# Which engine copies the first output bank out at the block boundaries of a Fourier layer fused with an ELU feed-forward

## The chip, the cores and the metric

The kernel runs on one core of a Trainium2 chip. The metric is device time in microseconds, the median of several executions. A core has TensorE (matrix products), VectorE, ScalarE and GpSimd (elementwise work), and SyncE, which here only issues DMAs. In the profile they are PE (with PEld for its weight loads), DVE, ACT, POOL and SP. [...]

## What is computed

A spectral layer on x (8 batches of 3008 tokens, 256 wide), followed by a feed-forward layer with an ELU (hidden width 2048):

```python
X = np.fft.rfft(x, axis=1)
Yr = Xr @ w_r - Xi @ w_i + b_r
Yi = Xr @ w_i + Xi @ w_r + b_i
Yr = np.sign(Yr) * np.maximum(np.abs(Yr) - 0.01, 0.0)   # Yi likewise
y = np.fft.irfft(Yr + 1j * Yi, n=3008, axis=1)

h = y @ w_in
g = np.where(h > 0.0, h, np.exp(np.minimum(h, 0.0)) - 1.0)
out = g @ w_out
```

## The kernel before

**Two streams of work in one loop.** The Fourier part of a batch is cut into some 38 "transform units": A and X (forward transform, the second after a trip through a scratch tensor in memory), M (the complex product and the soft threshold), B and Y (inverse transform, again with a scratch trip between them). The feed-forward layer of batch b is cut into 48 iterations: 6 blocks of 512 tokens (the last has 448) by 8 pairs of 128-wide slices of the hidden width. The main loop (line 826) runs over all 8 x 48 = 384 iterations, and each iteration of batch b also issues one transform unit of batch b+1 or b+2 as `plan` has laid it out. With r the iteration's number in its batch, an iteration without a unit is called `free` in the code; those are the last of each batch (r=41 among them) and nearly all of batch 7. The order of instructions on each engine is the order in which the code issues them; nothing reorders them later.

**One iteration i** issues, in this order:
1. its transform unit: matmuls into the PSUM tile `fps`, and a copy out of it, mostly by ScalarE (line 126). In an M unit, VectorE adds the bias (`yb`, line 196), and GpSimd does the soft threshold.
2. `front(i)`: four matmuls `hps` (line 688) into one of two PSUM tiles, the hidden activations of one pair for 512 tokens; then ScalarE computes the exponential into `Et` (line 701). Where the unit is an M unit (`on_act`), ScalarE does a Relu and an Exp instead (lines 698 and 699), which bound the exponential themselves.
3. `finish_elu()` for iteration i-1: one VectorE pass per pair gives `gT` from `hps` and `Et` (line 715, or 713 in the other form). It is the last reader of `hps`, so it frees that PSUM tile for `front(i+1)`, which is two iterations behind the one that it belongs to.
4. loads for later units (`f1`).
5. `elu(i)`: the minimum pass of VectorE over `Et` (line 726). There is none after Relu and Exp; in `free` iterations VectorE and GpSimd share it (line 724).
6. `back(i-2)`: eight matmuls (line 749) that add one pair's share of the output into two PSUM banks `ps_o`, the first four into the first bank, the other four into the second. When i-2 is the last pair of a block, `back` also copies both banks out into `osb` (line 763; line 767 for the short rows of the last block of a batch) and issues the output DMAs from SP (line 774).

**A block boundary** is thus an iteration i whose i-2 is the eighth pair of a block: r = 1, 9, 17, 25, 33 and 41, r=1 with the last block of the batch before. There are only two `ps_o` buffers, so the first matmuls of the next block, issued by `back(i-1)` one iteration later, must wait until the copies have emptied them. `osb` has two buffers as well; a copy into one waits until the output DMAs from two blocks earlier have read it.

At a boundary the units are, in batches 1 to 6: Y at r=1, X at r=9, M at r=17 and r=25, B at r=33. In batch 0 the list is one iteration later: X, B, Y, A at r = 9, 17, 25, 33. In batch 7 only r=1 has a unit.

Of the kernel before, what the change touches and what calls it, by code (L numbers as in the profile page):

```python
# [29 lines left out]
def kernel(  # L30
# [11 lines left out]
    nc = tc.nc  # L42
# [47 lines left out]
    NPAIR = NFT // 2  # L90
    NBLK = (S + TB - 1) // TB
    PER = NBLK * NPAIR
    LAG = 2
# [581 lines left out]
    def front(i, third, on_act):  # L675
        b, r = divmod(i, PER)
        blk, fp = divmod(r, NPAIR)
        bs = blk * TB
        nb = min(TB, S - bs)
        yT = yT_of[b]  # L680
        if third:
            hps = psF.tile([P, 2, TB], F32, name="hps", tag="fps")
        else:
            hps = psH.tile([P, 2, TB], F32, name="hps", tag="hps")
        for s in range(2):
            ft = 2 * fp + s
            for dt in range(2):
                nc.tensor.matmul(  # L688
                    hps[:, s, 0:nb], lhsT=w_in_s[:, dt, ft * P : ft * P + P],
                    rhs=yT[:, dt, bs : bs + nb], start=(dt == 0), stop=(dt == 1),  # L690
                )
        Et = late3.tile([P, 2, TB], F32, name="Et", tag="Et")
        E_ = Et[:, :, 0:nb]
        if i == n - 1:
            for s in range(2):
                nc.scalar.activation(E_[:, s], hps[:, s, 0:nb], AF.Exp)
        elif on_act:
            nc.scalar.activation(E_, hps[:, :, 0:nb], AF.Relu, scale=-1.0)  # L698
            nc.scalar.activation(E_, E_, AF.Exp, scale=-1.0)  # L699
        else:  # L700
            nc.scalar.activation(E_, hps[:, :, 0:nb], AF.Exp)  # L701
        return hps, Et, nb
# [3 lines left out]
    def finish_elu():  # L706
        for i, hps, Et, nb, whole in late_elu:
            E_, h_ = Et[:, :, 0:nb], hps[:, :, 0:nb]
            gT = late3.tile([P, 2, TB], F32R, name="gT", tag="gT")
            for s in range(2) if i == n - 1 else (slice(0, 2),):  # L710
                o, h, e = gT[:, s, 0:nb], h_[:, s], E_[:, s]
                if whole:
                    nc.vector.scalar_tensor_tensor(o, e, -1.0, h, ALU.add, ALU.max)  # L713
                else:
                    nc.vector.scalar_tensor_tensor(o, h, 0.0, e, ALU.max, ALU.add)  # L715
            g_of[i] = gT
        late_elu.clear()

    def elu(i, hps, Et, nb, on_pool, on_act):

        E_ = Et[:, :, 0:nb]
        if on_pool:
            for eng, s in ((nc.gpsimd, 1), (nc.vector, 0)):
                eng.tensor_scalar(E_[:, s], E_[:, s], 1.0, 0.0, ALU.min, ALU.max)  # L724
        elif not on_act:
            nc.vector.tensor_scalar(E_, E_, 1.0, -1.0, ALU.min, ALU.add)  # L726
        late_elu.append((i, hps, Et, nb, on_pool or on_act))

    def back(i):
        b, r = divmod(i, PER)  # L730
        blk, fp = divmod(r, NPAIR)
        bs = blk * TB
        nb = min(TB, S - bs)
        gT = g_of.pop(i)
        nsub = (nb + P - 1) // P
        if fp == 0:
            po_of[b, blk] = [
                psO.tile([P, 2, E], F32, name="ps_o", tag="outp") for _ in range((nsub + 1) // 2)
            ]
        po = po_of[b, blk]  # L740
        nq = (nsub + 1) // 2
        order = [(q, s) for q in range(nq) for s in range(2)]
        if i == n - 1:
            order = [(q, s) for s in range(2) for q in range(nq)]
        for q, s in order:
            ft = 2 * fp + s
            for i_ in range(2 * q, min(2 * q + 2, nsub)):
                t0, t1 = i_ * P, min(i_ * P + P, nb)
                nc.tensor.matmul(  # L749
                    po[q][0 : t1 - t0, i_ % 2, :], lhsT=gT[:, s, t0:t1],  # L750
                    rhs=w_out_r[:, ft, :], start=(ft == 0 and i_ % 2 == 0),
                    stop=(ft == NFT - 1), skip_group_check=True,
                )
        if fp < NPAIR - 1:
            return
        osb = late2.tile([P, 4, E], F32, name="osb", tag="osb")
        ov = out[b * S : b * S + S, :].rearrange("(r w j) e -> w r j e", w=4, j=8)
        last = i == n - 1
        for q in range(nq):
            k = min(2, nsub - 2 * q)  # L760
            copy = nc.vector.tensor_copy if last and q else nc.scalar.copy
            if nb >= (2 * q + k) * P:
                copy(osb[:, 2 * q : 2 * q + k, :], po[q][:, 0:k, :])  # L763
            else:
                for e in range(k):
                    rows = min(P, nb - (2 * q + e) * P)
                    copy(osb[0:rows, 2 * q + e, :], po[q][0:rows, e, :])
            for i_ in range(2 * q, 2 * q + k):
                t, end = bs + i_ * P, min(bs + i_ * P + P, bs + nb)
                while t < end:  # L770
                    w, r0 = t // WT, t % WT // 8
                    t1 = min(end, (w + 1) * WT)
                    p0, n8 = t - bs - i_ * P, (t1 - t) // 8
                    (nc.scalar if last and i_ % 2 == 0 else nc.sync).dma_start(
                        ov[w, r0 : r0 + n8], osb[p0 : p0 + 8 * n8, i_, :]
                    )
                    t = t1
        del po_of[b, blk]
# [4 lines left out]
    def plan(b):  # L783

        f0 = [[] for _ in range(PER)]
        f1 = [[] for _ in range(PER)]
        n1, n2 = b + 1, b + 2
        mid = [("X", u) for u in range(8)] + [
# [4 lines left out]
        ]  # L793
        if n1 < B:
            lead, seq = int(b == 0), [("y", u) for u in range(2, 6)] + mid
            seq.insert(20, ("y", 6))
            seq.insert(24, ("y", 7))
            xs = (3, 8, 13)
            yn = (45, 47)
        else:  # L800
            lead, seq = 0, [("y", u) for u in range(2, 8)]
        for t, u in enumerate(seq, lead):
            if u[0] == "y":
                f0[t].append(put("Y", b, u[1]))
            elif u[0] == "A":
                if n2 < B:
                    f0[t].append(put("A", n2, u[1]))
            else:
                f0[t].append(put(u[0], n1, *u[1:]))
            if u == ("A", 2):  # L810
                f1[t] += [(load_Bs, (n1, w)) for w in range(4)]
            if u == ("A", 5) and n2 < B:
                f1[t] += [(load_Z, (n2, s0, s1)) for s0, s1 in ((0, 8), (8, NS))]
        if b == 0:
            f1[xs[0]].append((lambda: gate(Z_of[1][:, 16, 0:1]), ()))
        if n2 < B:
            for ci in range(3):
                f1[xs[ci]].append((load_x, (n2, ci)))
        if n1 < B:
            for u in range(2):  # L820
                f0[yn[u]].append(put("Y", n1, u))
        return f0, f1
# [3 lines left out]
    for i in range(n + LAG):  # L826
        if i < n:
            r = i % PER
            if r == 0:
                f0, f1 = plan(i // PER)  # L830
                used = [bool(u0 or u1) for u0, u1 in zip(f0, f1)]
            free = not used[r]
            bare = bare + 1 if free else 0
            calm = free and (i >= n - 2 or (r + 2 < PER and not used[r + 1] and not used[r + 2]))
            for f, a in f0[r]:
                f(*a)
            on_act = any(f is unit_M for f, a in f0[r])
            h = front(i, calm and bare % 3 == 2, on_act)
        finish_elu()
        if i < n:  # L840
            for f, a in f1[r]:
                f(*a)
            elu(i, *h, free and i > 0, on_act)
        if i >= LAG:
            back(i - LAG)


# [28 lines left out]
```

## Time and profile before

| | |
|---|---|
| median of 3 executions | 930.38 us (930.08 to 931.6) |
| the profiled execution | 931.51 us |
| its span in the trace | 929.7 us |
| copies of line 763 on ScalarE | 88 of 128x512, 0.587 us on average |
| copies of line 767 on ScalarE, on VectorE | 14 on ScalarE, 2 on VectorE (last block) |
| granted TensorE clock | 0.998 |

The profile is a record of one execution. Its page gives the busy time of each engine and the costliest groups of instructions (line, engine, operation, output and inputs, count, then busy time and mean length in ns, then the idle time of the engine before them and what ended it). The list of waits names, for each engine and line, whose completion ended its idle time, in total, how often, and the longest. A timeline has the start in us from the beginning of the span, the length in us, the engine, the line, the operation, and in brackets the idle time of that engine in front of it with what ended it; neighbouring instructions of one kind are merged (x8), and their length is then from the first start to the last end. The ends of matmuls are modelled and they overlap, so that the distances between starts are the better measure on TensorE.

### The profile page before, as it was taken

The numbers are of one execution on the slowest core, as the hardware profiler recorded it, in microseconds if no ns is written. First come the engines' busy times: TensorE is split into PE (matmuls) and PEld (weight loads), VectorE is DVE, ScalarE is ACT, GpSimd is POOL, SyncE is SP. The second block draws the span as 40 slices with busy tenths as digits, with TensorE's granted clock in tenths as the row PEclk, the third lists the DMA queues.
The fourth block names the chain that finished last, engine by engine and source line by source line (L and its number), as shares of the span: only waits on it lengthen the run. The fifth ranks groups of instructions, "written<-read, shape, count | busy, mean of one in ns | idle before, by whom it ended". The sixth has DMA issues, their size and how long they took to land.

```text
span 929.7 us, 16768 instructions
## 1 busy us (share of the span) xinstructions
PE 909.2 (98%) x6583; PEld 644.4 (69%) x6583; DVE 734.5 (79%) x863; ACT 710.7 (76%) x818; POOL 267.9 (29%) x352
## 2 busy tenths in 40 slices
PE   8879999999999999999999999999999999999997
PEld 3447677776677666776677766777667766677775
DVE  7868778877788767886778877887778876888997
ACT  6657887787878788688787878778787878676654
POOL 6801441133310431205412153113331043321332
PEclk9999999999999999999999999999999999999999
DMA  8984216621383224722166021752138002421011
GB/s 264 353 254 136 91 47 187 196 69 46 95 223 111 69 65 126 224 84 86 51 181 202 24 91 46 222 161 68 47 94 224 22 24 63 116 51 43 23 46 43
DMA packets 90655, 106.21 MB, mean 114 GB/s; under 512 B 5264, under 2 KB 81296, under 8 KB 87216
## 3 DMA queue, kind: packets, MB, share of 16 engines
q1 hardware_dynamic: 84320, 77.61, 29.8%
q0 software_dynamic: 5968, 27.26, 8.9%
q8 instruction: 51, 0.84, 0.4%
q10 hardware_dynamic: 288, 0.26, 0.1%
q14 instruction: 28, 0.23, 0.1%
HBM read 55.31 MB, written 49.81 MB: 113 GB/s over the span
## 4 chain that ended last, share of the span: by engine, by line
PE 75%; DVE 14%; DMA 4%; ACT 4%; issue 1%; SPq 1%; DVEq 0%; POOL 0%; ACTq 0%; POOLq 0%
PE ps_o L749 30%; PE hps L688 29%; PE mps L189 8%; DVE gT L713 8%; DVE Et L724 3%; PE bps L238 2%; PE aps L143 2%; PE xps L174 2%; DMA Z<-DA 2%; DVE gT L715 1%; PE yps L276 1%; ACT Et L701 1%; DMA DA<-A 1%; DVE Et L726 1%; DMA xt<-in_x_dram 1%
## 5 line engine op out<-in xcount | busy, mean ns | idle before, releaser
L749 PE MATMUL ps_o<-w_out_r,gT 128*128 128x256 f32 (+1 forms) x3072 | 485.8, 301 | 0.8 <-DVE gT L713 0.5
L749 PEld LDWEIGHTS ps_o<-w_out_r,gT 128*128 128x128 f32 (+1 forms) x3072 | 406.4, 186 | 65.5 <-DVE gT L713 14.4
L688 PE MATMUL hps<-yT,w_in_s 128*128 128x512 bf16 (+1 forms) x1536 | 390.5, 376 | 5.4 <-DVE gT L715 2.7
L701 ACT ACTIVATE Et<-hps 128x1024 f32<-128x1024 f32 (+1 forms) x299 | 301.4, 1008 | 84.4 <-PE hps L688 80.4
L713 DVE SCALAR_TENSOR_TENSOR gT<-Et,hps 128x1024 fp32r<-128x1024 f32 (+2 forms) x187 | 219.9, 1176 | 62.9 <-ACT Et L699 41.6
L715 DVE SCALAR_TENSOR_TENSOR gT<-hps,Et 128x1024 fp32r<-128x1024 f32 (+1 forms) x198 | 240.1, 1213 | 17.6 <-DVE Et L726 0.9
L688 PEld LDWEIGHTS <-w_in_s 128*128 128x128 bf16 x1536 | 131.8, 98 | 141.0 <-issue 24.0
L726 DVE TENSOR_SCALAR Et<-Et 128x1024 f32<-128x1024 f32 (+1 forms) x198 | 136.0, 687 | 58.0 <-ACT Et L701 51.4
L204 POOL TENSOR_SCALAR clip<-yb 128x512 f32<-128x512 f32 x84 | 51.7, 615 | 335.1 <-DVE yb L196 234.5
L724 POOL TENSOR_SCALAR Et<-Et 128x512 f32<-128x512 f32 (+1 forms) x102 | 64.3, 630 | 271.1 <-ACT Et L701 269.9
L698 ACT ACTIVATE Et<-hps 128x1024 f32<-128x1024 f32 x84 | 86.4, 1029 | 70.0 <-PE hps L688 70.0
L205 POOL TENSOR_TENSOR Y<-yb,clip 128x512 bf16<-128x512 f32 x84 | 107.3, 1278 | 7.0
L196 DVE TENSOR_TENSOR yb<-mps,bias_bc 128x512 f32<-128x512 f32 x96 | 65.7, 687 | 39.3 <-PE mps L189 32.4
L699 ACT ACTIVATE Et<-Et 128x1024 f32<-128x1024 f32 x84 | 88.8, 1058 | 2.7
L126 ACT CAST yT<-yps 128x752 bf16<-128x752 f32 x63 | 49.7, 788 | 13.4 <-PE yps L276 13.4
L126 ACT CAST XT<-xps 128x768 bf16<-128x768 f32 x61 | 49.1, 807 | 13.7 <-PE xps L174 13.7
L189 PE MATMUL mps<-wcat_r,XT 128*128 128x512 bf16 x192 | 58.1, 384 | 0.6 <-ACT XT L126 0.6
L189 PE MATMUL mps<-wcat_s,XT 128*128 128x512 bf16 x192 | 57.1, 379 | 0.0
L126 ACT CAST A<-aps 128x1024 bf16<-128x1024 f32 x45 | 45.5, 1013 | 14.3 <-PE aps L143 11.9
L724 DVE TENSOR_SCALAR Et<-Et 128x512 f32<-128x512 f32 (+1 forms) x102 | 55.6, 545 | 0.4 <-ACT Et L701 0.2
L189 PEld LDWEIGHTS <-XT 128*128 128x128 bf16 x384 | 30.3, 98 | 29.5 <-ACT XT L126 0.9
L763 ACT COPY osb<-ps_o 128x512 f32<-128x512 f32 x88 | 47.2, 587 | 2.8 <-PE ps_o L749 2.8
(103 smaller groups left out, 398.5 us busy)
## 6 DMA issues: line engine op xcount, KB each, us to landing
xt<-in_x_dram POOLq DMA_DIRECT2D x21, 1024.0 KB, 5.2
out_dram<-osb SPq DMA_DIRECT2D x158, 128.0 KB
Bs<-DB SPq DMA_DIRECT2D x32, 384.0 KB
DA<-A SPq DMA_DIRECT2D x21, 512.0 KB
DB<-Bz SPq DMA_DIRECT2D x21, 512.0 KB
Z<-DA SPq DMA_DIRECT2D x7, 1152.0 KB
Z<-DA SPq DMA_DIRECT2D x11, 384.0 KB
xt<-in_x_dram POOLq DMA_DIRECT2D x6, 512.0 KB, 6.4
```

The source lines that it names most:

```text
L126: nc.scalar.copy(dst, src)
L189: nc.tensor.matmul(ps, lhsT=XT[:, dt, c, o : o + P], rhs=wm[:, dt, :], start=(m == 0 and dt == 0), stop=(m == 1 and dt == 1),)
L205: nc.gpsimd.tensor_tensor(Y_of[b, q][:, i, :], yb[:], clip[:], ALU.subtract)
L688: nc.tensor.matmul(hps[:, s, 0:nb], lhsT=w_in_s[:, dt, ft * P : ft * P + P], rhs=yT[:, dt, bs : bs + nb], start=(dt == 0), stop=(dt == 1),)
L698: nc.scalar.activation(E_, hps[:, :, 0:nb], AF.Relu, scale=-1.0)
L699: nc.scalar.activation(E_, E_, AF.Exp, scale=-1.0)
L701: nc.scalar.activation(E_, hps[:, :, 0:nb], AF.Exp)
L713: nc.vector.scalar_tensor_tensor(o, e, -1.0, h, ALU.add, ALU.max)
L715: nc.vector.scalar_tensor_tensor(o, h, 0.0, e, ALU.max, ALU.add)
L724: eng.tensor_scalar(E_[:, s], E_[:, s], 1.0, 0.0, ALU.min, ALU.max)
L726: nc.vector.tensor_scalar(E_, E_, 1.0, -1.0, ALU.min, ALU.add)
L749: nc.tensor.matmul(po[q][0 : t1 - t0, i_ % 2, :], lhsT=gT[:, s, t0:t1], rhs=w_out_r[:, ft, :], start=(ft == 0 and i_ % 2 == 0), stop=(ft = ...
```

## The change

At a boundary that is not `free`, and has a transform unit therefore, `back(i-2)` is issued before `elu(i)` and not after it, and its copy of the first bank goes to VectorE. The copies of the second bank stay on ScalarE. The boundaries of free iterations, and the first iterations, are as before.

```diff
-    def back(i):
+    def back(i, split):
...
-            copy = nc.vector.tensor_copy if last and q else nc.scalar.copy
+            copy = nc.vector.tensor_copy if (last and q) or (split and q == 0) else nc.scalar.copy
...
             for f, a in f1[r]:
                 f(*a)
+            split = not free and i > LAG and (i - LAG) % NPAIR == NPAIR - 1
+            if split:
+                back(i - LAG, True)
             elu(i, *h, free and i > 0, on_act)
-        if i >= LAG:
-            back(i - LAG)
+        else:
+            split = False
+        if i >= LAG and not split:
+            back(i - LAG, False)
```

By the instruction order of the two programs, the copies of 128x512 that move from ScalarE to VectorE are 35. On VectorE each stands directly behind the `gT` pass of iteration i-1, ahead of the minimum pass of i or, where there is none, ahead of the next `yb`. Of the instructions on TensorE, GpSimd and SP, the number and the order stay as they are.

## The prediction

> **What bounds the kernel now.** I read the page's busy times first, then the list of waits, then the timeline around the block boundaries.
>
> ```profile
> span 929.7 us, 16768 instructions
> ...
> PE 909.2 (98%) x6583; PEld 644.4 (69%) x6583; DVE 734.5 (79%) x863; ACT 710.7 (76%) x818; POOL 267.9 (29%) x352
> ...
> L763 ACT COPY osb<-ps_o 128x512 f32<-128x512 f32 x88 | 47.2, 587 | 2.8 <-PE ps_o L749 2.8
> ```
>
> TensorE sets the time. VectorE and ScalarE have some 20% free over the span, but an edit to either of them counts only where TensorE waits for it. So the question is which TensorE waits begin or end at the 35 boundaries where the new branch is taken.
>
> ```profile
> PEld ps_o L749 <- ACT osb L763: 7.7, 18, 0.5
> ...
> PE hps L688 <- DVE gT L715: 2.7, 10, 0.9
> ```
>
> These two rows of the list of waits matter (total, count, longest). In the first, the output matmuls of the next block wait until a copy has emptied the bank that they overwrite. In the second, the first matmuls of an iteration wait for the VectorE pass that frees their hidden bank. The first wait is what the change can remove; the second is what it can lengthen.
>
> The 35 boundaries are of three kinds. The branch is taken where the iteration's place r in its batch is 1, 9, 17, 25 or 33 (at 41 there is no transform unit), not in the last batch beyond r=1, and not at the very first r=1. That is 7 + 7 + 7 + 7 + 7. **Kind M:** r=17 and r=25 of batches 1 to 6, 12 boundaries, whose unit is an M; there ScalarE does Relu and Exp, and there is no minimum pass on VectorE. **Kind E (early):** all of r=1 and r=9, 14 boundaries with a Y or X unit. **The rest:** 9 boundaries. Below, i is the boundary iteration, which issues `back(i-2)` for the last pair of its block.
>
> **Kind M, where a wait goes away.** Timeline of one of them (columns: start, length, engine, line):
>
> ```profile
> 211.81 1.21 DVE L715 SCALAR_TENSOR_TENSOR gT<-hps,Et 128x1024 fp32r<-128x1024 f32 x1
> ...
> 213.34 1.03 PE L688 MATMUL hps<-yT,w_in_s 128*128 128x512 bf16 x4
> 213.61 0.69 DVE L196 TENSOR_TENSOR yb<-mps,bias_bc 128x512 f32<-128x512 f32 x1 [0.59 <-PE mps L189]
> 213.74 1.06 ACT L763 COPY osb<-ps_o 128x512 f32<-128x512 f32 x2
> 214.22 1.21 DVE L713 SCALAR_TENSOR_TENSOR gT<-Et,hps 128x1024 fp32r<-128x1024 f32 x1
> ...
> 214.36 1.02 PEld L749 LDWEIGHTS ps_o<-w_out_r,gT 128*128 128x128 f32 x8 [0.49 <-ACT osb L763]
> ...
> 216.06 0.55 PEld L688 LDWEIGHTS <-w_in_s 128*128 128x128 bf16 x4 [0.21 <-issue]
> ```
>
> ScalarE's two copies can only start at 213.74, behind Relu and Exp. The weight load of the next block starts at 214.36, some 0.04 us after the first copy ends (213.74 plus 0.59, the mean of L763). The second copy ends at 214.80, while the matmuls already run: the wait is for the first bank alone. What it costs TensorE is less than the 0.49 of the weight load, since matmuls are still running then. An iteration with the same kinds of work and no such wait gives the measure:
>
> ```profile
> 205.56 1.03 PE L688 MATMUL hps<-yT,w_in_s 128*128 128x512 bf16 x4
> ...
> 206.24 1.27 PE L749 MATMUL ps_o<-w_out_r,gT 128*128 128x256 f32 x8
> ...
> 207.98 0.55 PEld L688 LDWEIGHTS <-w_in_s 128*128 128x128 bf16 x4 [0.21 <-issue]
> ```
>
> From hidden matmuls to hidden matmuls it is 2.42 us there and 2.72 at the boundary: the wait costs 0.30.
>
> After the change the first bank's copy is on VectorE behind gT(i-1), which starts at 211.81. Passes of VectorE overlap by some 0.08 (213.61 + 0.69 is 214.30, and the next starts at 214.22), so a pass of 1.22 us is followed 1.14 after its start, and the copy starts at 212.95. Its price has no row of its own; the nearest are these, by line and form:
>
> ```profile
> L249 DVE CAST A<-bps 128x512 bf16<-128x512 f32 x1 | 0.7, 691 | 1.1 <-ACT A L248 1.1
> ...
> L767 DVE COPY osb<-ps_o 128x256 f32<-128x256 f32 x1 | 0.4, 424 | 0.8 <-PE ps_o L749 0.8
> ```
>
> L249 reads the same 128x512 of the same kind of bank and differs in its output type only; I take its 0.69. As a slot (start to the next start) that is 0.60 to 0.61, as 213.61 to 214.22 shows for the 0.69 us pass of L196. The bounds: from below 0.42, the copy of half the size, and from above 1.14, the slot of a pass over twice the columns.
>
> The copy then ends at 213.64, and the yb pass at 213.61 loses nothing (212.95 + 0.60 = 213.55). TensorE could start the output matmuls 0.68 after 213.34, as at 206.24: at 214.02, with the first bank already free. ScalarE's copy of the second bank ends at 213.74 + 0.59 = 214.33; the fifth of eight matmuls needs it at about 214.02 + 4 x 0.14 = 214.58 (0.14 being the pace of 8 matmuls in the 1.27 us row less one of about 0.3). So the wait goes and no other takes its place: 12 x 0.30 = 3.6 us gained.
>
> [...]
>
> **Kind E, where the copy stands in front of the minimum pass.** One r=1 boundary:
>
> ```profile
> 284.31 1.29 PE L749 MATMUL ps_o<-w_out_r,gT 128*128 128x256 f32 x8
> 284.40 1.23 DVE L715 SCALAR_TENSOR_TENSOR gT<-hps,Et 128x1024 fp32r<-128x1024 f32 x1
> ...
> 285.62 0.58 ACT L763 COPY osb<-ps_o 128x512 f32<-128x512 f32 x1
> ...
> 285.76 0.69 DVE L726 TENSOR_SCALAR Et<-Et 128x1024 f32<-128x1024 f32 x1
> 285.79 1.03 PE L688 MATMUL hps<-yT,w_in_s 128*128 128x512 bf16 x4
> 286.09 0.64 ACT L767 COPY osb<-ps_o 128x256 f32<-128x256 f32 x2
> ...
> 286.56 1.22 DVE L715 SCALAR_TENSOR_TENSOR gT<-hps,Et 128x1024 fp32r<-128x1024 f32 x1
> 286.62 0.80 ACT L126 CAST yT<-yps 128x752 bf16<-128x752 f32 x1
> 287.29 1.04 ACT L701 ACTIVATE Et<-hps 128x1024 f32<-128x1024 f32 x1
> ...
> 287.59 0.51 PE L276 MATMUL yps<-M,Bs 96*128 96x94 bf16 x8
> ...
> 287.93 1.03 PE L688 MATMUL hps<-yT,w_in_s 128*128 128x512 bf16 x4
> ...
> 288.36 0.69 DVE L726 TENSOR_SCALAR Et<-Et 128x1024 f32<-128x1024 f32 x1 [0.58 <-ACT Et L701]
> ...
> 289.00 1.03 ACT L701 ACTIVATE Et<-hps 128x1024 f32<-128x1024 f32 x1
> 289.16 1.23 DVE L715 SCALAR_TENSOR_TENSOR gT<-hps,Et 128x1024 fp32r<-128x1024 f32 x1
> 289.75 0.52 PE L174 MATMUL xps<-M,Z 96*128 96x96 bf16 x8
> ...
> 290.30 0.68 DVE L726 TENSOR_SCALAR Et<-Et 128x1024 f32<-128x1024 f32 x1
> 290.44 1.02 PE L688 MATMUL hps<-yT,w_in_s 128*128 128x512 bf16 x4 [0.18 <-DVE gT L715]
> ```
>
> The bank is complete in time: four of the eight matmuls at 284.31 are done before 285.0, while VectorE is in gT(i-1). The copy starts at 284.40 + 1.14 = 285.54 (289.16 to 290.30 is this 1.14), the minimum pass at 286.14 instead of 285.76, and everything behind it on VectorE, first gT(i), is 0.38 later: gT(i) ends at 288.16 instead of 287.78. It frees the bank for the hidden matmuls two iterations on, which start at 287.93, only 0.15 behind it; a pass that is waited for is followed 0.05 after its end (289.16 + 1.23 to 290.44). So these matmuls start at 288.21: 0.28 lost. r=9 has the same gap:
>
> ```profile
> 193.49 1.22 DVE L715 SCALAR_TENSOR_TENSOR gT<-hps,Et 128x1024 fp32r<-128x1024 f32 x1
> ...
> 194.86 1.03 PE L688 MATMUL hps<-yT,w_in_s 128*128 128x512 bf16 x4
> ```
>
> 14 x 0.28 = 3.9 us lost.
>
> Against this stands what leaves ScalarE. Today its two copies push the yT cast to 286.62 and Exp(i+1) to 287.29, the minimum pass behind it waits 0.58, and gT(i+1) ends so late that the hidden matmuls at 290.44 stall. They come 0.69 after the transform unit at 289.75, against 0.34 without a stall (287.59 to 287.93): 0.35 lost. With one copy fewer (its slot is 286.09 - 285.62 = 0.47) Exp(i+1) could start at 286.82, and not before 286.86, 1.07 after its matmuls (287.93 to 289.00). It ends at 287.90; VectorE is free at 286.94 + 1.14 = 288.08, so gT(i+1) starts 0.80 later, at 288.88, and ends at 290.11, ahead of the 290.38 at which TensorE, itself 0.28 late, wants the bank (290.44 - 0.34 + 0.28). This stall is gone. It follows all seven r=1 boundaries and the r=9 of batch 0 (8 of the 10 in the second row of the waits); after the other r=9 an M unit covers it. 8 x 0.34 = 2.7 us gained.
>
> **What costs nothing.** At r=33 VectorE idles before the minimum pass:
>
> ```profile
> 253.51 0.69 DVE L726 TENSOR_SCALAR Et<-Et 128x1024 f32<-128x1024 f32 x1 [0.42 <-ACT Et L701]
> ...
> 255.98 1.04 PE L688 MATMUL hps<-yT,w_in_s 128*128 128x512 bf16 x4
> ```
>
> Of the 0.60 slot some 0.5 falls into that idle time and the 0.08 of overlap, and gT(i), ending at 255.53 (253.51 + 0.80 + 1.22), has 0.45 before it is missed. Without this cover each would lose like kind E, 9 x 0.28 = 2.5. The wait in front of the copy gets longer, since it must also know that the old output DMAs of its buffer have landed; ScalarE's copy carries the same conditions today and started at 285.62 without idling. Extra conditions show up as short instructions of VectorE's queue:
>
> ```profile
> L767 DVEq EVENT_SEMAPHORE  x4: 49/50/50, 923.1 to 923.3; - x4
> ```
>
> ```profile
> 922.98 1.15 DVE L713 SCALAR_TENSOR_TENSOR gT<-Et,hps 128x448 fp32r<-128x448 f32 x2
> ```
>
> They ran beside the passes in front of them, so I take nothing for them; exposed, three of them would add 0.15 at each E boundary, 2.1 us. TensorE's, GpSimd's and SP's orders do not change: scratch writes, loads and output DMAs follow each other as now, and no copy ends more than a few hundredths later than today (at the r=1 boundary 285.54 + 0.69 = 286.23 against 285.62 + 0.58 = 286.20), so no output DMA is held up.
>
> **The sum.** 3.9 - 3.6 - 2.7 = -2.4 us. It is made against the profiled execution, whose span of 929.7 us lies in an execution of 931.51, 1.1 above the median of 930.38; on the median it gives 928.0.
>
> **The rivals.**
> First, **the copy fits** at kind E, because Exp(i) ends later than VectorE's free time suggests or the copy's slot is near the lower bound of 0.42, with 0.20 of delay and 0.10 lost. Then 1.4 - 3.6 - 2.7 = -4.9: 925.5; with no loss at all -6.3: 924.1. Against it: VectorE goes from gT(i-1) to the minimum pass with 0.22 to spare at most.
> [...]
> Third, **the wait at kind M stays**, because the first output matmul waits for both banks and the second still comes from ScalarE at 214.33. Then only kind E counts: 3.9 - 2.7 = +1.2, 931.6, no change. Against it: matmuls began at 214.36 with the second copy still running.
> Fourth, kind E loses and **the stall at 290.44 stays**, because the delay on VectorE passes on to gT(i+1): 3.9 - 3.6 = +0.3, 930.7.
>
> **How the numbers follow.** The forecast 0.48, the copy fits 0.17, slower 0.15, the wait at M stays 0.08, the stall stays 0.12. About 0.2%, 1.9 us, is what a measurement can tell from no change: faster ends at 928.5. The forecast's own spread, by a slot 0.05 shorter to 0.10 longer, is -3.1 to -1.0: two thirds of it is faster, 0.33, and with the copy that fits 0.50. The rest of the forecast, the stall and the wait at M give 0.34 for no change; slower takes 0.16. The range goes from the copy that fits, 925.0, to just above the third rival, 932.0; it leaves out most of the slower case and the largest gain.
>
> **What would show it.** Right: L763 splits into some 53 copies on ScalarE and 35 on VectorE of about 0.69 us; the wait of ps_o L749 for L763 falls from 18 to 6, those of the last batch; TensorE waits for gT L715 about 14 times instead of 8, one iteration earlier (near 288.2 instead of 290.4); minimum passes at r=1 and r=9 start 0.38 later behind gT(i-1). Wrong: a copy on VectorE far from 0.69, idle VectorE in front of it, or hidden matmuls at r=3 and r=11 that do not wait.

## The result, and the profile after

The changed kernel takes 926.49 us (926.0 to 927.33, 5 runs) against 930.66 for the kernel before (930.08 to 931.97, 5 runs): a ratio of 0.9953, with a 95% interval of 0.9940 to 0.9967. That is 4.2 us faster, inside the predicted range and in the predicted direction, where -2.4 us had been forecast. The profiled execution of the changed kernel took 927.22 us, with a span 4.3 us shorter than before. Its page begins:

```profile
span 925.4 us, 16719 instructions
...
PE 898.0 (97%) x6477; PEld 643.8 (70%) x6583; DVE 754.0 (81%) x898; ACT 697.3 (75%) x783; POOL 268.3 (29%) x352
```

VectorE has 35 instructions more and ScalarE 35 fewer. (PE has 6477 records against 6583 weight loads: 106 matmul records are missing.) The view of line 763 in the changed kernel (least, median and greatest length in ns, first and last start):

```profile
L763 ACT COPY osb<-ps_o x53: 566/585/607, 81.6 to 920.5; 128x512 f32<-128x512 f32 x53
L763 DVE COPY osb<-ps_o x35: 680/681/683, 81.5 to 831.9; 128x512 f32<-128x512 f32 x35
```

The copy's price was taken from a related pass as 0.69 us; it is 0.681 on VectorE, against 0.585 for the copies that stay on ScalarE. The two rows of the list of waits that the prediction started from are now:

```profile
PEld ps_o L749 <- ACT osb L763: 1.7, 5, 0.4
...
PE hps L688 <- DVE gT L715: 1.4, 2, 0.9
```

The waits for the bank went from 18 to 5, all of them at boundaries of free iterations, which the change does not touch. The waits for gT fell from 10 to 2.

**An M boundary after the change** (timeline):

```profile
212.71 0.68 DVE L763 COPY osb<-ps_o 128x512 f32<-128x512 f32 x1
...
213.11 1.03 PE L688 MATMUL hps<-yT,w_in_s 128*128 128x512 bf16 x4
213.38 0.69 DVE L196 TENSOR_TENSOR yb<-mps,bias_bc 128x512 f32<-128x512 f32 x1
...
213.51 0.57 ACT L763 COPY osb<-ps_o 128x512 f32<-128x512 f32 x1
213.76 1.10 PEld L749 LDWEIGHTS ps_o<-w_out_r,gT 128*128 128x128 f32 x8
...
215.53 0.55 PEld L688 LDWEIGHTS <-w_in_s 128*128 128x128 bf16 x4 [0.21 <-issue]
```

VectorE's copy ends at 213.39, before the weight load of the next block at 213.76, which has no wait in brackets any more. From the hidden matmuls to the weight load of the next ones it is 2.42 us instead of 2.72.

**An r=1 boundary after the change** (timeline, VectorE and TensorE with ScalarE's copy and Exp):

```profile
283.35 1.23 DVE L715 SCALAR_TENSOR_TENSOR gT<-hps,Et 128x1024 fp32r<-128x1024 f32 x1
...
284.50 0.68 DVE L763 COPY osb<-ps_o 128x512 f32<-128x512 f32 x1
284.60 0.63 ACT L767 COPY osb<-ps_o 128x256 f32<-128x256 f32 x2
...
284.74 1.03 PE L688 MATMUL hps<-yT,w_in_s 128*128 128x512 bf16 x4
285.09 0.68 DVE L726 TENSOR_SCALAR Et<-Et 128x1024 f32<-128x1024 f32 x1
...
285.81 1.23 DVE L715 SCALAR_TENSOR_TENSOR gT<-hps,Et 128x1024 fp32r<-128x1024 f32 x1
285.81 1.03 ACT L701 ACTIVATE Et<-hps 128x1024 f32<-128x1024 f32 x1
...
286.56 0.51 PE L276 MATMUL yps<-M,Bs 96*128 96x94 bf16 x8
...
287.09 1.02 PE L688 MATMUL hps<-yT,w_in_s 128*128 128x512 bf16 x3
...
288.89 0.52 PE L174 MATMUL xps<-M,Z 96*128 96x96 bf16 x8
...
289.24 1.03 PE L688 MATMUL hps<-yT,w_in_s 128*128 128x512 bf16 x4
```

Copy and minimum pass start 1.15 and 1.74 after the start of gT(i-1) at 283.35, as worked out (1.14, and 1.14 + 0.60). gT(i) ends at 287.04, and the hidden matmuls start 0.05 later, at 287.09, which is 0.53 after their transform unit instead of 0.34: they waited. The list of waits doesn't show it, because the modelled end of the unit's matmuls (286.56 + 0.51 = 287.07) covers the gap. From 284.74 to 287.09 it is 2.35 us, before 2.14 (285.79 to 287.93): 0.21 lost. From there to the next hidden matmuls, the stall of the kernel before is gone: 2.15 us (287.09 to 289.24) against 2.51 (287.93 to 290.44), 0.36 gained. All seven r=1 boundaries show this pair, 0.19 to 0.20 lost and 0.33 to 0.37 gained.

### The profile page after: what moved, and what is told of

Read it like the earlier page. It is cut to its first block, busy times and chain, and to the rows that moved or that the text cites. A ratio compares the mean times of both kernels' runs of the same rounds, so it can differ in the third digit from the quotient of the medians.

```text
span 925.4 us, 16719 instructions
## 1 busy us (share of the span) xinstructions
PE 898.0 (97%) x6477; PEld 643.8 (70%) x6583; DVE 754.0 (81%) x898; ACT 697.3 (75%) x783; POOL 268.3 (29%) x352
## 4 chain that ended last, share of the span: by engine, by line
PE 72%; DVE 16%; ACT 3%; issue 3%; DMA 3%; POOL 1%; SPq 0%; DVEq 0%; ACTq 0%; POOLq 0%
PE ps_o L749 29%; PE hps L688 28%; PE mps L189 8%; DVE gT L713 7%; DVE Et L724 3%; PE bps L238 2%; DVE gT L715 2%; ACT Et L701 2%; PE yps L276 2%; PE aps L143 2%; DVE Et L726 2%; PE xps L174 1%; DMA Z<-DA 1%; DMA DA<-A 1%; DMA xt<-in_x_dram 1%
## 5 line engine op out<-in xcount | busy, mean ns | idle before, releaser
L688 PE MATMUL hps<-yT,w_in_s 128*128 128x512 bf16 (+1 forms) x1463 | 383.5, 375 | 8.6 <-DVE gT L715 1.4
L715 DVE SCALAR_TENSOR_TENSOR gT<-hps,Et 128x1024 fp32r<-128x1024 f32 (+1 forms) x198 | 240.3, 1214 | 15.5
L189 PE MATMUL mps<-wcat_s,XT 128*128 128x512 bf16 x183 | 55.2, 379 | 1.1
L189 PE MATMUL mps<-wcat_r,XT 128*128 128x512 bf16 x171 | 53.5, 385 | 0.7 <-ACT XT L126 0.6
L251 ACT CAST Bz<-bps 128x1024 bf16<-128x1024 f32 x46 | 45.9, 999 | 3.2 <-PE bps L238 3.2
```

Source lines behind the costliest of these rows:

```text
L189: nc.tensor.matmul(ps, lhsT=XT[:, dt, c, o : o + P], rhs=wm[:, dt, :], start=(m == 0 and dt == 0), stop=(m == 1 and dt == 1),)
L688: nc.tensor.matmul(hps[:, s, 0:nb], lhsT=w_in_s[:, dt, ft * P : ft * P + P], rhs=yT[:, dt, bs : bs + nb], start=(dt == 0), stop=(dt == 1),)
```

## The experiments

Two theories were put against each other first. P is the prediction's: TensorE gains where it waited for the first bank, and loses or gains by small amounts where the copy stands ahead of the minimum pass. R: what counts is ScalarE's relief, an equal share for each copy that leaves it. All ratios are to the kernel before, with a 95% interval. The diffs are against the changed kernel.

**e1, the M boundaries alone.**

```diff
             split = not free and i > LAG and (i - LAG) % NPAIR == NPAIR - 1
+            split = split and on_act
```

> VectorE copies the first bank at the 12 boundaries with an M unit alone; the other 23 are as before. Theory P (the prediction's): each of the 12 gives back the 0.30 us for which TensorE waited on the bank, -3.6 us, about 927.1, and the wait of ps_o L749 for L763 falls from 18 to about 6. Theory R (the gain is ScalarE's relief, an equal share of the 4.2 us for each of the 35 copies moved): 12 x 0.12 = -1.4 us, about 929.2.

Measured: 927.39 us, ratio 0.9965 (0.9951 to 0.9978). The row of the list of waits falls as with the whole change:

```profile
PEld ps_o L749 <- ACT osb L763: 1.5, 5, 0.4
```

Twelve moved copies bring 3.3 us of the 4.2. P holds; R's 1.4 is far off.

**e2, the boundaries r=1 and r=9 alone.**

```diff
             split = not free and i > LAG and (i - LAG) % NPAIR == NPAIR - 1
+            split = split and r in (1, 9)
```

> The new order and VectorE's copy at r=1 and r=9 alone. Theory P: eight boundaries lose 0.2 us and give back the 0.35 us stall three iterations on, six lose 0.2 us and give nothing back: 8 x -0.15 + 6 x 0.22 = +0.1 us, no change, about 930.8; the 12 waits for L763 at M boundaries stay. Theory R: 14 x 0.12 = -1.7 us, about 929.0.

Measured: 930.43 us, ratio 0.9995 (0.9987 to 1.0004): fourteen moved copies bring nothing. List of waits:

```profile
PEld ps_o L749 <- ACT osb L763: 7.6, 17, 0.5
...
PE hps L688 <- DVE gT L715: 1.2, 2, 0.9
```

The 12 waits for the bank at M boundaries are all among the 17, and the eight stalls on gT are gone all the same; what they gave back was lost at the boundary. Loss and gain cancel, as P has it.

**e3, the change without r=9 of batches 1 to 6,** the boundaries that lose and give nothing back.

```diff
             split = not free and i > LAG and (i - LAG) % NPAIR == NPAIR - 1
+            split = split and not (r == 9 and i > PER)
```

> The change without the six r=9 boundaries of batches 1 to 6. Theory P: they are where it loses, 6 x 0.22 us; without them -4.2 - 1.3 = -5.5 us, about 925.2, some 1.3 us better than the change. Theory R: six copies fewer, -4.2 + 0.7 = -3.5 us, about 927.2.

Measured: 926.03 us, ratio 0.9947 (0.9934 to 0.9959). The direction is P's, but the times differ too little from the change's for the intervals to tell them apart. In the traces the loss is plain. The changed kernel at r=9:

```profile
192.27 1.03 PE L688 MATMUL hps<-yT,w_in_s 128*128 128x512 bf16 x4
...
194.63 1.02 PE L688 MATMUL hps<-yT,w_in_s 128*128 128x512 bf16 x4
```

and the kernel before, whose second row (194.86) the prediction shows:

```profile
192.72 1.03 PE L688 MATMUL hps<-yT,w_in_s 128*128 128x512 bf16 x4
```

It is 2.36 us against 2.14: 0.22 lost. In e3, where the copy is back on ScalarE, it is 2.15:

```profile
191.14 1.03 PE L688 MATMUL hps<-yT,w_in_s 128*128 128x512 bf16 x4
...
193.29 1.03 PE L688 MATMUL hps<-yT,w_in_s 128*128 128x512 bf16 x4
```

The same 0.22 us is saved in each of batches 1 to 6.

**e4, the other bank.** VectorE copies the second bank and ScalarE the first.

```diff
-            copy = nc.vector.tensor_copy if (last and q) or (split and q == 0) else nc.scalar.copy
+            copy = nc.vector.tensor_copy if (last and q) or (split and q == 1) else nc.scalar.copy
```

> Same order, but VectorE copies the second bank (or its short rows) and ScalarE the first. Theory P: at the M boundaries ScalarE's copy of the first bank still begins behind Relu and Exp, so the 12 waits of ps_o L749 for L763 stay with 0.49 us each, and only what happens at the other boundaries is left: -0.5 us, about 930.1. Theory R: the same number of copies leaves ScalarE, -4.2 us, about 926.5, as with the change.

Measured: 929.2 us, ratio 0.9981 (0.9972 to 0.9989), between the two. But P's reason failed: the 12 waits did not stay. Timeline of an M boundary of e4:

```profile
213.08 0.68 DVE L763 COPY osb<-ps_o 128x512 f32<-128x512 f32 x1
...
213.89 0.57 ACT L763 COPY osb<-ps_o 128x512 f32<-128x512 f32 x1
214.13 1.10 PEld L749 LDWEIGHTS ps_o<-w_out_r,gT 128*128 128x128 f32 x8
```

ScalarE's copy runs to 214.46, and the next block begins at 214.13 without a wait. The built program says why: at M boundaries its first output matmul waits for VectorE, the fifth for ScalarE.

```
L749 Matmult ps_o_2642<-w_out_r_65,gT_2605 128x256 [waits DVE_49]
L749 Matmult ps_o_2643<-w_out_r_65,gT_2605 128x256 [waits Activation_49]
```

The pool gave the next block the bank that VectorE had copied as its first. Which bank is "first" is thus not fixed by the kernel's code, but by the pool when the program is built. What e4 lost against the change was at r=1 and r=9: 0.37 and 0.30 us from start to start, where the change loses 0.20 and 0.22. Two things may make the difference, which no run tried apart: the second bank is complete later (at the r=1 boundary shown above, the eighth output matmul ends at 284.56, the fourth at 284.09), and at r=1 its short rows are two copies (of 128x256 and 64x256, 0.38 us each by the median on ScalarE in the kernel before). In e5 the pool can't choose.

**e5, e4 with fixed banks.**

```diff
-        tc.tile_pool(name="psO", bufs=2, space=bass.MemoryType.PSUM, reuse_waits="tile")
+        tc.tile_pool(name="psO", bufs=1, space=bass.MemoryType.PSUM, reuse_waits="tile")
...
-                psO.tile([P, 2, E], F32, name="ps_o", tag="outp") for _ in range((nsub + 1) // 2)
+                psO.tile([P, 2, E], F32, name="ps_o", tag=f"outp{q}") for q in range((nsub + 1) // 2)
```

> As e4 (VectorE copies the second bank, ScalarE the first), but each of the two banks has a pool of its own with one buffer, so that the first bank of the next block is always the one that ScalarE copied. Theory P with a pool that hands out whichever bank is released first: in e4 the next block at an M boundary began in VectorE's bank, so the wait was gone there too; with fixed banks it comes back, 12 x 0.30 = +3.6 us over e4's 929.2, about 932.8, and the waits of ps_o L749 for L763 are 17 or 18 again. Theory R (ScalarE's relief is what counts): as e4, about 929.2.

Measured: 932.14 us, ratio 1.0014 (1.0005 to 1.0023), 2.9 us above e4 and slower than the kernel before. The list of waits and the M boundary of e5:

```profile
PEld ps_o L749 <- ACT osb L763: 7.5, 17, 0.5
```

```profile
213.63 0.57 ACT L763 COPY osb<-ps_o 128x512 f32<-128x512 f32 x1
214.25 1.00 PEld L749 LDWEIGHTS ps_o<-w_out_r,gT 128*128 128x128 f32 x8 [0.49 <-ACT osb L763]
```

The wait is back with its old 0.49 us, and the time with it. From start to start, e5 is slower than e4 by 0.27 to 0.28 us at each of the 12 M boundaries, and after the first iterations nowhere else by as much as 0.1, so the fixed banks cost nothing of their own. As many copies leave ScalarE as in the change, so R is out: what counts is that the bank in which the next block begins is emptied early.

**e6, the same copies behind the minimum pass.**

```diff
-            if split:
-                back(i - LAG, True)
             elu(i, *h, free and i > 0, on_act)
+            if split:
+                back(i - LAG, True)
```

> VectorE copies the first bank at the same 35 boundaries, but behind its minimum pass. Theory P: nothing changes at the M boundaries (-3.6 us). Where there is a minimum pass the copy starts 0.60 behind it, some 286.36 in the r=1 boundary of the trace before, ends at 287.04, and the next block's matmuls, due at 286.47, wait 0.6 for the bank; less the 0.35 stall that goes at eight boundaries, it is 8 x 0.25 + 6 x 0.6 + 9 x 0.45 = +9.7 us, together +6 us, about 936.7. Rival: only the time that the copy takes on VectorE counts, not its place: within 0.5 us of the change, 926.5.

Measured: 928.6 us, ratio 0.9983 (0.9974 to 0.9992). Neither: 2 us worse than the change, and 8 better than worked out. Timeline at r=1:

```profile
284.01 0.69 DVE L726 TENSOR_SCALAR Et<-Et 128x1024 f32<-128x1024 f32 x1
...
284.62 0.68 DVE L763 COPY osb<-ps_o 128x512 f32<-128x512 f32 x1
284.69 1.19 PEld L749 LDWEIGHTS ps_o<-w_out_r,gT 128*128 128x128 f32 x8
```

The copy has hardly begun, and the next block starts without a wait. The pool again: in the built program of e6 the next block begins in ScalarE's bank at all 23 boundaries that have a minimum pass, and in VectorE's at the 12 others. (In the changed kernel it is VectorE's at all 35.)

**e9, e6 with fixed banks** (the pool as in e5).

> As e6 (VectorE's copy behind its minimum pass), with a pool of one buffer for each of the two banks, so that the next block must begin in the bank that VectorE copies. If e6 lost little only because the pool gave the next block ScalarE's bank first, the wait that was worked out for e6 comes now: some 0.3 us more than in e6 at 14 boundaries and 0.4 at nine, +8 us over e6's 928.6, about 936.6, and about 23 waits of ps_o L749 for VectorE's L763. Rival (the place of the copy doesn't matter): as e6, 928.6.

Measured: 934.93 us, ratio 1.0041 (1.0027 to 1.0055), 6.3 us above e6. List of waits, then r=1, both of e9:

```profile
PEld ps_o L749 <- DVE osb L763: 17.1, 23, 1.1
```

```profile
286.70 0.68 DVE L763 COPY osb<-ps_o 128x512 f32<-128x512 f32 x1
...
287.44 0.99 PEld L749 LDWEIGHTS ps_o<-w_out_r,gT 128*128 128x128 f32 x8 [0.78 <-DVE osb L763]
```

The 23 waits are the 14 + 9 that were counted; 8 us over e6 had been expected. So the place ahead of the minimum pass does matter, as long as the next block begins in VectorE's bank; and e6 lost little because the pool moved it.

**e7, less VectorE time behind the copy:** at r=1 and r=9 GpSimd takes half of the minimum pass.

```diff
-            elu(i, *h, free and i > 0, on_act)
+            elu(i, *h, (free and i > 0) or (split and r in (1, 9)), on_act)
```

> The change, and at r=1 and r=9 GpSimd takes half of the minimum pass (line 724), as in free iterations. Theory P: the loss there is the 0.2 us by which gT(i) ends late; VectorE's half is some 0.2 us shorter than the whole pass, and GpSimd's half (0.63 us from the end of Exp) is done by then, so gT(i) starts about 0.2 earlier: 14 x -0.2 = -2.8 us against the change, about 923.7. Rival: GpSimd's half ends later than VectorE's whole pass did, and nothing or a little is lost, 926.5 to 928.

Measured: 925.49 us, ratio 0.9948 (0.9935 to 0.9960): by the medians 1.0 us below the change, by the intervals not apart from it. Timeline at r=1:

```profile
283.22 0.61 POOL L724 TENSOR_SCALAR Et<-Et 128x512 f32<-128x512 f32 x1 [5.70 <-ACT Et L701]
283.55 0.56 DVE L724 TENSOR_SCALAR Et<-Et 128x512 f32<-128x512 f32 x1
...
284.21 1.22 DVE L713 SCALAR_TENSOR_TENSOR gT<-Et,hps 128x1024 fp32r<-128x1024 f32 x1
```

Half the columns took VectorE 0.56 us here. Without GpSimd beside it such a pass took 0.42 in batch 7 of e8:

```profile
852.09 0.42 DVE L724 TENSOR_SCALAR Et<-Et 128x512 f32<-128x512 f32 x1
```

The 0.2 expected had taken GpSimd's half to be done when VectorE's begins. It was not: it ran to 283.83, and VectorE's half, begun at 283.55, ended 0.28 after that. Of the 0.12 that is saved (0.56 against 0.68), half is lost again in front of gT(i), which in the built program waits for GpSimd and VectorE now, with a queue instruction of 21 ns for the second wait. The view of line 713 between 283 and 286 us:

```profile
L713 DVEq EVENT_SEMAPHORE  x1: 21/21/21, 284.1 to 284.1; - x1
```

So gT(i) starts 0.10 after the end of the pass instead of 0.04, and 0.66 after its start instead of 0.72. That is 0.06 for each of 14 boundaries, 0.8 us in all.

**e8, the change at the boundaries of free iterations too.**

```diff
-            split = not free and i > LAG and (i - LAG) % NPAIR == NPAIR - 1
+            split = i > LAG and i < n - 2 and (i - LAG) % NPAIR == NPAIR - 1
```

> The change at the boundaries of free iterations too (12 more: r=41 of batches 0 to 6, and five in batch 7). There TensorE waits for gT in nearly every iteration, so theory P has the copy's 0.6 us on VectorE delay gT by 0.5 to 0.6 and gives back the 0.2 to 0.4 us waits for ScalarE's copy: 12 x +0.25 = +3 us against the change, about 929.5. Rival: VectorE has room there too, since GpSimd shares the minimum pass: -0.2 us each, about 924.

Measured: 931.39 us, ratio 1.0011 (1.0002 to 1.0019): all of the gain is gone, 0.4 us for each of the 12 boundaries added. List of waits, then the timeline at an r=41:

```profile
PEld ps_o L749 <- DVE osb L763: 4.7, 8, 0.6
```

```profile
269.15 0.69 DVE L763 COPY osb<-ps_o 128x512 f32<-128x512 f32 x1
...
269.89 0.94 PEld L749 LDWEIGHTS ps_o<-w_out_r,gT 128*128 128x128 f32 x8 [0.59 <-DVE osb L763]
```

Without a transform unit the next block comes so soon that it waits for VectorE's copy itself, at eight of the 12 boundaries (4.7 us in all, 0.59 at this one). That is not the loss that P expected, a late gT. P's loss stands at the other four, in batch 7, where the pool gives the next block ScalarE's bank: behind the first of them the output matmuls wait 0.53 us for gT.

**e10, e3 and e7 together, and e11, the change again beside it.**

> e3 and e7 together: the six r=9 boundaries of batches 1 to 6 as before the change, and at the other eight boundaries with a Y or X unit GpSimd takes half of the minimum pass. By e3 and e7: -1.3 us against the change for the six, and 8 x -0.07 = -0.6 for the eight, about 924.7.

> The change once more, beside e10 on the same chip: 926.5, and 0.5 to 1% below neither; e10 some 1.9 us faster.

Measured on one chip: e10 925.46 us (924.75 to 926.21), ratio 0.9937 (0.9923 to 0.9950); e11 926.99 us (926.67 to 927.71), ratio 0.9955 (0.9943 to 0.9968). The ranges of their runs don't meet: e10 is 1.5 us faster than the change. From start to start the traces differ as e3 and e7 say, by 0.22 at six boundaries and 0.06 at eight, 1.8 us.

## Why the prediction was right, point by point

The time is nearer to the first rival (925.5) than to the forecast (928.0), but not by the rival's reason, a delay of 0.20 at the minimum pass: the delay was 0.38. The mechanism is the forecast's, with one term that was too large and one gain that it did not have.

**What bounds the kernel** and **kind M** held as written: 12 x 0.30 = 3.6 us, of which e1 by itself measured 3.3. The third rival (the first matmul waits for both banks) is refuted by e4, where it started at 214.13 while ScalarE's copy ran to 214.46. The mark of "18 to 6, those of the last batch" was one off: of the six, five were in the last batch, and the sixth, at r=33 of batch 6, went with the change. Of the five after, four are in the last batch and one at an r=41.

**Kind E** had the right mechanism and a term of the wrong size. The bank was complete at 285.13, the modelled end of the fourth output matmul, and not before 285.0, but still ahead of the copy at 285.54. The delay of 0.38 at the minimum pass was right; the loss is some 0.21 us instead of 0.28, 14 x 0.07 = 1.0 us in all. The step that was off is "everything behind it on VectorE is 0.38 later": gT(i) follows the minimum pass 0.72 after its start (285.09 to 285.81), where the trace before has 0.80 (285.76 to 286.56). A queue instruction of 21 ns is missing there. The view of line 715 between 284 and 288 us, the kernel before and then the changed one:

```profile
L715 DVEq EVENT_SEMAPHORE  x2: 21/21/21, 284.3 to 286.5; - x2
```

```profile
L715 DVEq EVENT_SEMAPHORE  x1: 21/21/21, 287.7 to 287.7; - x1
```

By the order of the two programs, gT(i) waited for TensorE and for the minimum pass; since the copy in front of it has waited for later matmuls already, the built program leaves the first wait out. That this is where the 0.07 us come from fits, and so does e7, where the instruction is back and gT(i) starts 0.06 later behind the end of the pass; but no run tried it alone.

**The stall that goes** was worth 0.36 instead of 0.34, and e2 shows that it goes even where nothing else is gained.

**"What costs nothing"** was wrong in sign at r=33: there was a small stall of the same kind that I had not looked for. Hidden matmuls of the kernel before (from 255.98, shown in the prediction) and of the changed one:

```profile
258.40 1.02 PE L688 MATMUL hps<-yT,w_in_s 128*128 128x512 bf16 x4
```

```profile
254.97 1.04 PE L688 MATMUL hps<-yT,w_in_s 128*128 128x512 bf16 x4
...
257.23 1.04 PE L688 MATMUL hps<-yT,w_in_s 128*128 128x512 bf16 x4
```

2.42 us before, 2.26 after: 0.16 gained in each of batches 1 to 5, some 0.8 us. ScalarE's Exp comes earlier there too: behind r=33 it starts 1.11 us after its hidden matmuls instead of 1.55. In batch 6, where the iteration after r=33 has no unit, 0.15 is lost instead (2.46 us against 2.31), because gT ends later and is waited for (the row of the hidden matmuls has 0.50 us of idle time in front of it, 0.34 before).

With the sizes of the traces the sum is 14 x 0.21 - 12 x 0.30 - 8 x 0.36 - 5 x 0.16 + 0.15 = -4.2 us, against 4.3 by which the spans differ. The case "slower", with 0.15 of the chances, did not come: the copy's slot at r=1 was 0.59 us (284.50 to 285.09). That a copy on VectorE can hold TensorE up is seen in e8, where it waited 8 times, up to 0.6 us, and in e9, 23 times, up to 1.1 us. The fourth (the stall stays) fell with e2. The mark "about 14 waits for gT L715 near 288.2" was a bad one: the waits are there, but hidden under modelled ends, and only distances between starts show them.

## What to carry to other kernels

Where TensorE is the bound, ask for each boundary which instruction ends its wait, and move only what stands in front of that one: 12 of the 35 moved copies gave 3.3 of the 4.2 us. VectorE was idle for 21% of the span before the change and had 0.15 us of slack at the r=1 boundary: measure the slack at the place where the work is put, from start to start. When a copy changes engine, look up which buffer the pool hands out next, because the wait may move to another bank than the code suggests, as in e4 and e6.

## What the runs showed of the hardware that was not expected

A VectorE pass of line 724 over 512 columns took 0.42 us with GpSimd idle (e8, eight passes of 0.415 to 0.420), against 0.68 for line 726 over 1024. Where it began while GpSimd's pass over the other half was running, it ended 0.28 us after GpSimd's (e7, 57 passes, 0.277 to 0.283), with lengths from 0.46 to 0.88: these passes gained nothing by starting earlier. Where VectorE began first (e7, nine passes), its pass took 0.43 us and GpSimd's 0.84 to 0.85 instead of 0.61. In the changed kernel gT of line 715 followed its minimum pass 0.72 us after that pass's start in 21 of 22 places with no queue instruction of 21 ns in between, and 0.79 or 0.80 in 127 of 141 with one.
